# Linear attention and a gated feed-forward layer on one core: the same steps in another order, with more two-operand work on GpSimd

## The chip, the cores and the metric

The kernel runs on one core of one Trainium2 chip. Its time is the device time of one execution in microseconds (us), the median of several runs. Five engines share the work, and each takes its own instructions strictly in the order in which they were written: TensorE (PE, matrix products into PSUM), VectorE (DVE), ScalarE (ACT), GpSimd (POOL) and SyncE (SP, which here only issues transfers). An instruction that waits holds up everything behind it on its engine.

## The reference

The inputs are q, k, v of shape (8, 8, 576, 64), three weight matrices and a vector of 512 gains.

```
q_s = softmax(q, axis=-1)                      # over the 64 features of a head
k_s = softmax(k, axis=2)                       # over the 576 positions
kv  = einsum('bhsd,bhse->bhde', k_s, v)
att = einsum('bhsd,bhde->bhse', q_s, kv)       # -> x, (4608, 512)
xn  = x / sqrt(mean(x*x) + 1e-6) * rms_g
g   = xn @ w_gate                              # 512 -> 1536
out = (g * sigmoid(g) * (xn @ w_val)) @ w_out  # 1536 -> 512
```

All is float32. The kernel keeps the precision with 16-bit and reduced-precision products by splitting each operand into a high part (a cast) and a low part (the operand less its high part), and by adding three products of the parts.

## The kernel before

**Tiling.** The 4608 tokens are nine blocks of 512 (index j, 0 to 8). For every block the program computes the attention of its tokens in four groups of two heads (`q_...` steps, and for each of the eight sequences the `k_...`, `v_...` and `kv_...` steps), normalises the result (`n_...`, `x_nrm`), and sends it through the feed-forward layer. Blocks 0 and 1 are done in plain products (`f1`, `f1p`, `f2`), while the weights are loaded and converted. Blocks 2 to 8 use seven products in place of eight for a 2x2 split of the two input weight matrices, so sums and differences of quarters of the weights and of the tokens are formed first.

**The steps of a late block j**, by name:

- `n_rows.j` (L969) spreads the normalising factors over a tile, `x_nrm.j.g` (L849) multiplies four tiles by it, `x_sum.j.n` (L885 to L891) forms four sums of token quarters, `o_x_hi` casts them and `o_x_lo` (L905) forms the low parts. These are the moving operands of the seven products.
- `pp.j.u.n` (L1118) is one of the seven products for one of six slices u of the hidden width: 12 matmuls into one PSUM bank. There are only two such banks (pool `ps_gv`), so a product can start when the second-last one before it has been evicted.
- `ev.j.u.n` evicts and adds up: `ev` 0 on ScalarE, `ev` 1 to 6 on VectorE at L1137, `ev` 7 on VectorE at L1142; `ev` 8 and 9 are the two silu (L1145, ScalarE), `ev` 10 and 11 (L1148, VectorE) multiply gate and value, both then in SBUF.
- `hu_hi` (L402, ScalarE) and `hu_lo` (L1157) split the hidden values, `o_hi` (L402) and `o_lo` (L1000) the output weights. The tile of a low part is `hl` or `ol`, of a high part `hh` or `oh`.
- `fu.j.u.n.k` (L1170) adds the slice to the output, two matmuls each of (hh, oh), (hh, ol) and (hl, oh), in that order. `store` writes the block out.

Other steps that form a low part or a product of two tiles in SBUF are `q_sub` (L770), `q_mul` (L792), `q_lo` (L807), `x_acc` (L919), `n_lo` (L928), `w_lo` (L992), `b_lo` (L1073), `t_op` (L1081 to L1087), `t_lo` (L1099) and `h_lo` (L1228).

**What sets the order.** No loop and no scheduler at build time: a table of 3260 steps, `ORDER`, is read from first to last, and each step appends its instructions to its engines' queues. A step may carry a letter for its engine: `:A` ScalarE, `:D` VectorE, `:P` GpSimd. Many steps that read two operands from SBUF can run on either of the last two. All transfers are issued by SP, in the table's order.

```
    with tc.manual_schedule():
        for step in ORDER.split():
            step, _, engine = step.partition(":")
            name, *args = step.split(".")
            unit[0] = where[engine]
            steps[name](*map(int, args))
```

Of the kernel before, what the change touches and what calls it, by code (L numbers as in the profile page):

```python
# [23 lines left out]
exp_table constants k_load.0.0 q_load0.0.0 v_ones.0.0 kv_zero0.0 warm.9 v_ones.0.2 kv_zero0.1 k_load.0.2 v_ones.0.1  # L24
v_ones.0.3 v_load.0.0 kv_zero.4 kv_zero.5 warm.2.0 kv_zero.6 q_load0.0.3 k_max0.0.0 warm.2.1 kv_zero.7 warm.2.2
kv_zero.0 k_load.0.3 warm.2.10 kv_zero.1 q_max0.0.0 q_load0.0.1 kv_zero.2 k_tr.0.0 warm.2.11 k_top.0.0 kv_zero.3
warm.2.3 k_diag.0.0:A k_max0.0.2 q_sub0.0.0:P k_load.0.1 warm.2.12 v_load.0.2 k_rows.0.0 warm.2.5 k_sub.0.0 v_ones.1.0
v_ones.1.1 q_exp.0.0 warm.2.4 q_load0.0.2 warm.2.6 q_sum0.0.0 k_exp.0.0 warm.2.7 q_eps0.0.0 v_load.0.3 warm.2.8
q_rec0.0.0 q_max0.0.3 q_mul0.0.0:P k_mm.0.0 v_load.0.1 k_max0.0.3 k_tr.0.2 warm.2.9 q_sub0.0.3:P g_load k_top.0.2
k_tr.0.3 q_t0.0.0 load_w.0.0 k_eps.0.0 k_diag.0.2:A k_top.0.3 k_rec.0.0 load_w.0.1 q_exp.0.3 k_rows.0.2 q_max0.0.1  # L30
load_w.1.0 k_diag.0.3:A k_sub.0.2 q_sub0.0.1:P q_c0.0.0:A load_w.1.1 k_rows.0.3 k_load.1.0 kv_norm0.0.0:A k_max0.0.1
k_exp.0.2 k_sub.0.3 load_w.0.2 q_exp.0.1 k_mm.0.2 q_load0.1.0 q_sum0.0.3 k_exp.0.3 k_tr.0.1 q_x0.0.0 k_top.0.1
q_max0.0.2 k_diag.0.1:A k_mm.0.3 x_sq.0.0 load_w.2.0 q_sum0.0.1 q_sub0.0.2:P k_rows.0.1 load_w.2.1 n_sum0.0 k_eps.0.2
k_sub.0.1 load_w.1.2 q_exp.0.2 load_w.3.0 q_eps0.0.3 x_hi.0.0:A q_rec0.0.3 load_w.3.1 k_rec.0.2 q_mul0.0.3:P
q_eps0.0.1 load_w.3.2 k_eps.0.3 k_exp.0.1 x_lo.0.0 k_load.1.1 kv_norm0.0.2:A q_rec0.0.1 k_mm.0.1 k_rec.0.3
q_mul0.0.1:P q_sum0.0.2 conv_mul.0.0 q_t0.0.3 load_w.2.2 k_eps.0.1 conv_low.0.0.1 k_rec.0.1 conv_shift.0.0 q_t0.0.1
k_load.1.2 kv_norm0.0.3:A q_eps0.0.2 conv_sign.0.0 q_c0.0.3:A kv_norm0.0.1:A q_load0.1.1 q_rec0.0.2 q_x0.0.3
conv_add.0.0.1 g_abs conv_mul.0.1 q_c0.0.1:A conv_shift.0.1 q_mul0.0.2:P conv_low.0.1.1 q_x0.0.1 conv_sign.0.1
v_load.1.0 x_hi.0.3:A q_t0.0.2 conv_add.0.1.1 x_sq.0.3 x_lo.0.3 s_tr.0 x_sq.0.1 k_max.1.0 w_hi.0.0.2:A n_sum0.1
q_load0.1.2 s_top.0 q_c0.0.2:A f1.0.0.0.0 w_lo.0.0:P f1.0.1.0.0 w_lo.0.1:D s_rows.0 x_hi.0.1:A q_x0.0.2 s_bits.0  # L40
load_w.4.0 conv_low.1.0.2 f1.0.0.0.1 load_w.4.1 f1.0.1.0.1 q_max0.1.0 f1.0.1.0.3 v_load.1.1 f1.0.0.0.3 conv_mul.1.0
x_lo.0.1 q_sub0.1.0:P x_sq.0.2 conv_shift.1.0 x_hi.0.2:A n_sum0.2 conv_sign.1.0 conv_low.0.2.1 f1.0.0.0.2 x_lo.0.2
f1.0.0.1.0 conv_mul.1.1 n_sum0.3 q_exp.1.0 conv_shift.1.1 f1.0.1.0.2 f1.0.0.1.1 conv_low.2.0.2 conv_sign.1.1
f1.0.0.1.2 f1.0.1.1.0 f1.0.1.1.1 f1.0.0.1.3 n_t.0 conv_add.1.0.2 conv_mul.0.2 f1.0.0.2.0 f1.0.1.1.2 f1.0.0.2.1 n_y0.0
conv_low.1.2.1 f1.0.1.1.3 f1.0.0.2.2 conv_shift.0.2 f1.0.1.2.0 f1.0.1.2.1 f1.0.0.2.3 q_sum0.1.0 f1.0.1.2.2 f1.0.1.2.3
n_y1.0 w_hi.1.0.2:A load_w.5.0 load_w.5.1 conv_low.3.0.2 w_lo.1.0:P conv_sign.0.2 k_tr.1.0 n_rows.0 w_lo.1.1:P
conv_mul.2.0 k_top.1.0 conv_low.3.2.1 g_mul.0 conv_add.0.2.1 k_diag.1.0:A n_cols.0 f1.1.0 silu.0 q_eps0.1.0 q_rec0.1.0
k_max.1.1 load_w.4.2 q_mul0.1.0:P conv_low.2.2.1 q_load0.1.3 conv_shift.2.0 k_rows.1.0 h_mul.0 k_sub.1.0 f1.1.1
conv_sign.2.0 conv_mul.2.1 k_exp.1.0 g_mul.1 conv_shift.2.1 conv_mul.1.2 f2.0 silu.1 conv_sign.2.1 conv_shift.1.2
conv_mul.3.0 conv_add.2.0.2 conv_sign.1.2 conv_shift.3.0 conv_mul.3.1 conv_sign.3.0 conv_add.1.2.1 w_hi.2.0.2:A  # L50
load_w.6.0 h_mul.1 q_t0.1.0 load_w.6.1 q_max0.1.1 conv_low.4.0.2 w_lo.2.0:P f1.2.0 load_w.5.2 q_c0.1.0:D
conv_shift.3.1 conv_mul.3.2 w_lo.2.1:P k_max.1.2 q_sub0.1.1:P f1.2.1 conv_sign.3.1 conv_shift.3.2 q_exp.1.1
conv_add.3.0.2 conv_mul.2.2 g_mul.2 conv_low.5.0.2 conv_sign.3.2 f2.1 q_sum0.1.1 conv_mul.4.0 conv_add.3.2.1
load_w.7.0 conv_shift.2.2 w_hi.3.0.2:A load_w.7.1 conv_shift.4.0 load_w.7.2 conv_low.4.2.1 w_lo.3.0:P conv_sign.2.2
silu.2 conv_sign.4.0 k_mm.1.0 w_lo.3.1:P q_max0.1.2 conv_mul.4.1 f1.3.0 k_load.1.3 k_eps.1.0 h_mul.2 conv_add.2.2.1
conv_shift.4.1 k_rec.1.0 conv_low.6.0.2 v_ones.1.2 v_load.1.2 conv_sign.4.1 q_sub0.1.2:P f2.2 q_max0.1.3
kv_norm0.1.0:A conv_add.4.0.2 g_mul.3 conv_mul.4.2 load_w.6.2 q_eps0.1.1 conv_low.5.2.1 q_rec0.1.1 conv_shift.4.2
conv_mul.5.2 conv_sign.4.2 silu.3 q_sub0.1.3:P load_w.8.0 f1.3.1 conv_shift.5.2 w_hi.4.0.2:A load_w.8.1 conv_sign.5.2
conv_add.4.2.1 conv_mul.5.0 w_lo.4.0:D conv_low.7.0.2 w_lo.4.1:P conv_shift.5.0 load_w.8.2 q_x0.1.0 conv_sign.5.0
q_exp.1.2 conv_add.5.2.1 o_hi.4:A f1.4.0 q_sum0.1.2 conv_mul.5.1 h_mul.3 o_lo.4:P conv_low.7.2.1 load_w.10.2  # L60
conv_shift.5.1 o_hi.5:A conv_sign.5.1 q_exp.1.3 q_mul0.1.1:P f1.4.1 g_mul.4 conv_mul.6.0 o_lo.5:P q_sum0.1.3
q_load.2.0 silu.4 conv_shift.6.0 kv_hi.1.0:A x_sq.1.0 conv_add.5.0.2 conv_sign.6.0 conv_low.6.2.1 f2.3 h_mul.4
conv_mul.6.1 q_eps0.1.2 x_raw.1.0 conv_shift.6.1 h_hi.4:A conv_sign.6.1 kv_lo.1.0:P load_w.10.0 conv_mul.6.2 h_lo.4:P
q_rec0.1.2 load_w.10.1 s_max.0.0 w_hi.5.0.2:A k_tr.1.1 warm.2.13 conv_add.6.0.2 conv_low.8.0.2 k_top.1.1 f2.4
conv_shift.6.2 conv_sign.6.2 k_diag.1.1:A conv_low.8.2.1 w_lo.5.0:D conv_mul.7.0 w_lo.5.1:P s_max.2.0 w_hi.6.0.2:A
k_rows.1.1 f1.5.0 conv_add.6.2.1 k_sub.1.1 conv_low.10.2.1 k_max.1.3 k_exp.1.1 w_lo.6.0:P o_hi.6:A q_t0.1.1
conv_shift.7.0 o_lo.6:P f1.6.0 q_c0.1.1:D g_mul.5 conv_mul.7.1 w_lo.6.1:P conv_sign.7.0 silu.5 conv_low.10.0.2
conv_shift.7.1 q_mul0.1.2:P k_mm.1.1 conv_sign.7.1 f1.5.1 k_load.2.0 v_ones.1.3 k_eps.1.1 conv_mul.7.2 conv_add.7.0.2
# [1234 lines left out]
```

## Time and profile before

| | us |
|---|---|
| median of 3 runs (range) | 1038.28 (1038.12 to 1042.46) |
| the profiled execution | 1038.59 |
| its span, first to last instruction | 1036.8 |
| PE busy | 948.4 |
| VectorE busy | 860.3 |
| ScalarE busy | 594.7 |
| GpSimd busy | 460.2 |

The profile is of one execution. A row of a group view reads: line, engine, operation, written tile, read tiles, shapes, count, then total busy time and the mean of one in ns, then the idle time ahead of them and what ended it. A row of waits reads: engine and line that waited, engine and line waited for, total us, how many times, the longest. A row of the timeline reads: start, duration, engine, line, operation, tiles, count, and in brackets the engine's idle time ahead of it and what ended it. Lines are those of the kernel before; the table is one line longer in the changed kernel, so every line behind it there has a number higher by one.

### The profile page before, as it was taken

The numbers are of one execution on the slowest core, as the hardware profiler recorded it, in microseconds if no ns is written. First come the engines' busy times: TensorE is split into PE (matmuls) and PEld (weight loads), VectorE is DVE, ScalarE is ACT, GpSimd is POOL, SyncE is SP. The second block draws the span as 40 slices with busy tenths as digits, with TensorE's granted clock in tenths as the row PEclk, the third lists the DMA queues.
The fourth block names the chain that finished last, engine by engine and source line by source line (L and its number), as shares of the span: only waits on it lengthen the run. The fifth ranks groups of instructions, "written<-read, shape, count | busy, mean of one in ns | idle before, by whom it ended". The sixth has DMA issues, their size and how long they took to land.

```text
span 1036.8 us, 17459 instructions
## 1 busy us (share of the span) xinstructions
PE 948.4 (91%) x6418; PEld 735.5 (71%) x6418; DVE 860.3 (83%) x1564; ACT 594.7 (57%) x929; POOL 460.2 (44%) x386
## 2 busy tenths in 40 slices
...
DMA packets 129697, 57.82 MB, mean 56 GB/s; under 512 B 101796, under 2 KB 123596, under 8 KB 129612
## 3 DMA queue, kind: packets, MB, share of 16 engines
...
## 4 chain that ended last, share of the span: by engine, by line
DVE 39%; PE 34%; issue 6%; DMA 4%; ACT 4%; SPq 3%; POOL 1%; DVEq 0%; ACTq 0%
PE ps_gv L1118 19%; PE ps_o L1170 12%; SPq L687 3%; DVE w_br L1137 3%; DVE ol L1000 2%; DVE tm L1137 2%; DVE sw L759 2%; DVE x_raw L849 2%; DVE xo L905 2%; DMA qt<-in_q_dram 2%; DVE cm L562 1%; PE ps_gv L1197 1%; DVE wf L1137 1%; DVE w_br L1148 1%; DVE sm L778 1%
## 5 line engine op out<-in xcount | busy, mean ns | idle before, releaser
L1118 PEld LDWEIGHTS <-w_gv 128*128 128x128 f16 x2016 | 192.8, 99 | 47.6 <-issue 25.0
L1118 PE MATMUL ps_gv<-xo,w_gv 128*128 128x256 f16 x1296 | 157.8, 276 | 5.1 <-ACT xo L402 3.1
L402 ACT CAST oh<-w_o 128x512 fp32r<-128x512 f32 x104 | 64.1, 617 | 131.2 <-PE ps_o L1170 130.1
L1000 POOL TENSOR_TENSOR ol<-w_o,oh 128x512 fp32r<-128x512 f32 x44 | 57.7, 1311 | 129.1 <-ACT oh L402 128.8
L1170 PE MATMUL ps_o<-oh,hh 128*128 128x512 f32 x336 | 111.1, 412 | 3.2 <-ACT hh L402 3.2
L1170 PE MATMUL ps_o<-oh,hl 128*128 128x512 f32 x336 | 105.3, 394 | 2.4 <-DVE hl L1157 2.3
L1170 PE MATMUL ps_o<-ol,hh 128*128 128x512 f32 x336 | 105.2, 394 | 0.0
L1118 PEld LDWEIGHTS <-w_br 128*128 128x128 f16 x756 | 72.2, 98 | 25.8 <-issue 14.6
L1118 PE MATMUL ps_gv<-x_op,w_gv 128*128 128x256 f16 x720 | 87.4, 273 | 0.3 <-DVE tm L1137 0.3
L1000 DVE TENSOR_TENSOR ol<-w_o,oh 128x512 fp32r<-128x512 f32 x60 | 56.5, 942 | 37.3 <-ACT oh L402 37.3
L1185 PE MATMUL ps_gv<-xo,wf 128*128 128x512 f32 x288 | 76.5, 417 | 2.1 <-DVE tm L1212 2.0
L1170 PEld LDWEIGHTS ps_o<-oh,hl 128*128 128x128 f32 x336 | 62.7, 189 | 19.3 <-DVE hl L1157 5.2
L1118 PE MATMUL ps_gv<-xo,w_br 128*128 128x256 f16 x540 | 65.5, 273 | 9.8 <-DVE tm L1142 5.7
L1170 PEld LDWEIGHTS ps_o<-ol,hh 128*128 128x128 f32 x336 | 63.5, 189 | 14.3
L1118 PEld LDWEIGHTS <-wf 128*128 128x128 f16 x504 | 49.8, 101 | 29.2 <-issue 17.1
L1185 PEld LDWEIGHTS ps_gv<-xo,wf 128*128 128x128 f32 x288 | 55.1, 196 | 18.3 <-issue 2.7
L807 POOL TENSOR_TENSOR ql<-qT,qh 128x512 fp32r<-128x512 f32 x20 | 26.6, 1329 | 92.7 <-ACT qh L402 92.7
L1170 PEld LDWEIGHTS ps_o<-oh,hh 128*128 128x128 f32 x336 | 58.1, 190 | 12.6 <-ACT hh L402 3.5
L1137 DVE TENSOR_TENSOR tm<-ps_gv,tm 128x512 f32<-128x512 f32 x71 | 48.0, 682 | 12.1 <-PE ps_gv L1118 11.7
L1137 DVE TENSOR_TENSOR w_br<-ps_gv,w_br 128x512 f32<-128x512 f32 x71 | 48.0, 683 | 11.0 <-PE ps_gv L1118 10.9
L919 POOL TENSOR_TENSOR acc<-acc,sq 128x512 f32<-128x512 f32 x18 | 25.7, 1426 | 65.3 <-ACT sq L915 65.3
L1118 PE MATMUL ps_gv<-xo,wf 128*128 128x256 f16 x360 | 44.2, 276 | 9.3 <-DVE w_br L1142 3.3
...
## 6 DMA issues: line engine op xcount, KB each, us to landing
...
```

The costliest lines, as they stand in the source:

```text
L402: (e.copy if e is nc.scalar else e.tensor_copy)(dst, src)
L687: nc.sync.dma_start(qt[p0:p0 + 32, c0 // 32:c1 // 32], q[b, 2 * g + h, s0:s0 + c1 - c0, 32 * f:32 * f + 32].rearrange("(m c) i -> c m i", ...
L759: nc.vector.tensor_reduce(out=sw[32 * (a ^ 1):32 * (a ^ 1) + 32], in_=st[32 * a:32 * a + 32].unsqueeze(2), axis=AX.X, op=ALU.max)
L807: on(nc.gpsimd).tensor_tensor(out=ql, in0=qT_[j, g], in1=qh_[j, g][0].bitcast(F32), op=ALU.subtract)
L849: on(nc.vector).tensor_tensor(out=XR[:, g], in0=XR[:, g], in1=r_[j], op=ALU.mult)
L905: on(nc.gpsimd).tensor_tensor(out=x_as(j, m, xl), in0=x_part(j, m), in1=x_as(j, m, xo_[j, m][0]), op=ALU.subtract)
L919: on(nc.gpsimd).tensor_tensor(out=acc_[j], in0=acc_[j], in1=sq_[j, g], op=ALU.add)
L1000: on(nc.vector).tensor_tensor(out=ol, in0=WO_(s % NF), in1=wo_[s][0].bitcast(F32), op=ALU.subtract)
L1118: nc.tensor.matmul(pair(ps, i), lhsT=a[:, wt], rhs=y if i else y.rearrange("p (a c) -> p a c", a=2), start=(k == 0 and i == 0 and p == 0), ...
L1137: nc.vector.tensor_tensor(out=out, in0=b, in1=src[j, u], op=ALU.add)
L1170: nc.tensor.matmul(po[2 * n + t], lhsT=a[:, o:o + P], rhs=w, start=(u == 0 and i == 0 and p == 0), stop=(u == NU - 1 and i == 1 and p == 2))
L1185: nc.tensor.matmul(pd[s], lhsT=m[:, a, c * P:(c + 1) * P], rhs=X[j, c][x], start=(n == 1), stop=(n == 3 * NKT))
```

## The change

The steps are the same 3260, with the same arguments. Their order is new from the first row on, and some carry another letter. The order was written on the premise that the work of GpSimd and VectorE on two operands in SBUF uses one resource. No instruction is added to or removed from the computation itself. Of the diff, which replaces the whole table, the rows of one place (`...` where lines are left out):

```
-ev.5.5.2 n_rows.6 fu.5.4.1.1 ev.5.5.3 x_nrm.6.3:P x_nrm.6.1:D fu.5.4.0.0 x_nrm.6.0:D x_nrm.6.2:P q_t.7.1 o_x_hi.6.0
...
+pp.5.4.3 ev.5.4.9 ev.5.4.5 ev.5.4.11 pp.5.5.1 n_rows.6 ev.5.4.6 ev.5.5.0 x_nrm.6.2:P k_eps.7.0 pp.5.5.2 k_rec.7.0
+k_sub.7.1 kv_hi.7.0:A x_nrm.6.1:P kv_lo.7.0 k_exp.7.1 pp.5.5.6 ev.5.5.1 x_nrm.6.3:P k_top.7.2 ev.5.5.8 q_t.7.1
...
```

Counted over the table, the letters move as follows. A step with no letter runs on its default engine, the same in both.

| step | `:D` before, now | `:P` before, now |
|---|---|---|
| all | 254, 223 | 303, 334 |
| `hu_lo` (L1157) | 39, 11 | 45, 73 |
| `o_lo` (L1000) | 60, 57 | 44, 47 |
| `x_sum` (L885 to L891) | 1, 13 | 27, 15 |
| `x_nrm` (L849) | 16, 18 | 16, 14 |
| `t_op`, `t_lo` (L1081 to L1099) | 18, 9 | 30, 39 |
| `q_mul` (L792) | 24, 20 | 4, 8 |
| `b_lo`, `w_lo` (L1073, L992) | 16, 10 | 32, 38 |

ScalarE's queue gets 100 loads of an activation table in place of 82, since silu and exp alternate more often.

**Place 1: VectorE, the end of block 5 and the preparation of block 6.** The row at L1142 evicts the fourth product of slice 5 of block 5 and so frees a bank; r is the factor tile, x_raw the attention result, xo the low parts, ol a low part of the output weights. Before:

```order
L1137 TENSOR_TENSOR tm<-ps_gv,tm 128x512
L969 STREAM_TRANSPOSE r<-y 128x512
L1137 TENSOR_TENSOR w_br<-ps_gv,tm 128x512
L849 TENSOR_TENSOR x_raw<-x_raw,r 128x512 x2
L797 STREAM_TRANSPOSE qT<-qt 128x512
L905 TENSOR_TENSOR xo<-x_raw,xo 128x512
L1000 TENSOR_TENSOR ol<-w_o,oh 128x512
L905 TENSOR_TENSOR xo<-x_raw,xo 128x512
L1000 TENSOR_TENSOR ol<-w_o,oh 128x512
L1142 TENSOR_TENSOR w_br<-ps_gv,w_br 128x512
```

And in the changed kernel:

```order
L563 TENSOR_REDUCE cm<-kt 116x128
L1138 TENSOR_TENSOR w_br<-ps_gv,tm 128x512
L1143 TENSOR_TENSOR w_br<-ps_gv,w_br 128x512
L1149 SCALAR_TENSOR_TENSOR w_bx<-wf,ig,w_bx 128x512
L906 TENSOR_TENSOR xo<-sq,xo 128x512
L906 TENSOR_TENSOR xo<-x_raw,xo 128x512
L1158 TENSOR_TENSOR hl<-w_bx,hh 128x512
L1158 TENSOR_TENSOR hl<-tm,hh 128x512
L890 TENSOR_TENSOR sq<-sq,x_raw 128x512
L1138 TENSOR_TENSOR tm<-ps_gv,tm 128x512
```

The six two-operand instructions that stood between two evictions have left that place; the eviction at L1143 now follows its forerunner at once, and six others stand behind it, ahead of the next eviction.

**Place 2: VectorE, the same place one block later (end of block 6).** Before:

```order
L969 STREAM_TRANSPOSE r<-y 128x512
L1137 TENSOR_TENSOR tm<-ps_gv,w_bx 128x512
L849 TENSOR_TENSOR x_raw<-x_raw,r 128x512 x2
L797 STREAM_TRANSPOSE qT<-qt 128x512
L905 TENSOR_TENSOR x_op_94<-x_raw,x_op_94 128x512
L1000 TENSOR_TENSOR ol<-w_o,oh 128x512
L905 TENSOR_TENSOR xo<-x_raw,xo 128x512
L1000 TENSOR_TENSOR ol<-w_o,oh 128x512
L1142 TENSOR_TENSOR tm<-ps_gv,tm 128x512
```

And in the changed kernel:

```order
L1138 TENSOR_TENSOR tm<-ps_gv,w_bx 128x512
L906 TENSOR_TENSOR xo<-x_raw,xo 128x512 x2
L892 TENSOR_TENSOR sq<-x_raw,sq 128x512
L808 TENSOR_TENSOR ql<-qT,qh 128x512
L1001 TENSOR_TENSOR ol<-w_o,oh 128x512
L906 TENSOR_TENSOR xo<-sq,xo 128x512
L798 STREAM_TRANSPOSE qT<-qt 128x512
L1143 TENSOR_TENSOR tm<-ps_gv,tm 128x512
```

Here six two-operand instructions stand ahead of the eviction in both kernels; the factor tile and the multiplications by it have moved to an earlier place.

**Place 3: GpSimd, block 4, around the low parts of its slice 1** (hl with w_bx and tm). Before:

```order
L807 TENSOR_TENSOR ql<-qT,qh 128x512
L1157 TENSOR_TENSOR hl<-w_bx,hh 128x512
L558 MEMSET vt 116x10
L1000 TENSOR_TENSOR ol<-w_o,oh 128x512 x2
L919 TENSOR_TENSOR acc<-acc,sq 128x512
L1157 TENSOR_TENSOR hl<-w_br,hh 128x512
```

And in the changed kernel:

```order
L808 TENSOR_TENSOR ql<-qT,qh 128x512
L1158 TENSOR_TENSOR hl<-w_bx,hh 128x512
L1158 TENSOR_TENSOR hl<-tm,hh 128x512
L771 TENSOR_TENSOR qt<-qt,st 128x512
L1001 TENSOR_TENSOR ol<-w_o,oh 128x512
L920 TENSOR_TENSOR acc<-acc,sq 128x512
```

The second low part of the slice, which VectorE formed before, now stands behind the first one on GpSimd.

More of the change, by code (lines that the diff above doesn't have):

```diff
@@ L23 @@
 ORDER = """
[L24 to L68, printed above, removed]
```

547 lines of the change are left out of this document (296 added, 251 removed).

## The prediction, made before the changed kernel was run

> **What bounds the kernel now.** I read the busy times by stage first, then what TensorE waits for, then the timeline at the longest of those waits. Busy time of each engine in four stages:
>
> ```profile
> 0.00:150.00 150.00, 135.73 (x679) 97.93 (x680) 128.85 (x240) 114.41 (x173) 110.91 (x112) 0.97 0.66 183
> 150.00:350.00 200.00, 166.53 (x933) 106.25 (x932) 178.45 (x331) 140.81 (x219) 114.93 (x92) 0.92 0.18 42
> 350.00:850.00 500.00, 472.07 (x3603) 388.89 (x3601) 443.15 (x835) 280.97 (x442) 196.24 (x157) 0.99 0.16 38
> 850.00:1037.00 187.00, 174.03 (x1211) 142.40 (x1208) 109.83 (x160) 58.55 (x97) 38.15 (x27) 0.98 0.04 14
> sum 1037.00, PE 948.36 PEld 735.47 DVE 860.28 ACT 594.75 POOL 460.24; mean PE 237.09 PEld 183.87 DVE 215.07 ACT 148.69 POOL 115.06
> ```
>
> The columns are PE, PEld, DVE, ACT, POOL, then the granted clock. TensorE is the bound: busy 948.36 of 1037. A new order cannot shorten its matmuls, so all that can be won is its idle time, 88.6 us: 14.3 up to 150, 33.5 from 150 to 350, 27.9 from 350 to 850, 13.0 after that. VectorE is nearly full in the middle stages (178.45 of 200, 443.15 of 500), GpSimd is not. TensorE's own waits:
>
> ```profile
> PE ps_gv L1118 <- DVE tm L1142: 12.2, 7, 3.8
> PE ps_o L1244 <- ACT hh L402: 6.8, 1, 6.8
> PE ps_gv L1118 <- DVE w_br L1142: 5.3, 4, 3.3
> PE ps_gv L1118 <- DVE w_bx L1142: 4.1, 2, 3.3
> PE ps_gv L1118 <- ACT xo L402: 3.1, 1, 3.1
> PE ps_gv L1118 <- DVE wf L1142: 2.3, 3, 1.1
> PE ps_gv L1118 <- DVE xo L905: 2.1, 1, 2.1
> ```
>
> The reader is to see one line, L1142: the four rows that name it make 23.9 us in 16 waits. It is one eviction in each slice. Why is it late? VectorE, GpSimd and TensorE at the end of block 5:
>
> ```profile
> 714.17 3.12 DVE L849 TENSOR_TENSOR x_raw<-x_raw,r 128x512 f32<-128x512 f32 x2
> 717.97 1.28 DVE L905 TENSOR_TENSOR xo<-x_raw,xo 128x512 f16<-128x512 f32 x1
> 719.18 1.76 DVE L1000 TENSOR_TENSOR ol<-w_o,oh 128x512 fp32r<-128x512 f32 x1
> 720.86 1.64 DVE L905 TENSOR_TENSOR xo<-x_raw,xo 128x512 f16<-128x512 f32 x1
> 722.42 1.75 DVE L1000 TENSOR_TENSOR ol<-w_o,oh 128x512 fp32r<-128x512 f32 x1
> 724.09 0.68 DVE L1142 TENSOR_TENSOR w_br<-ps_gv,w_br 128x512 f32<-128x512 f32 x1
> ...
> 713.75 2.99 POOL L849 TENSOR_TENSOR x_raw<-x_raw,r 128x512 f32<-128x512 f32 x2 [1.73 <-DVE r L969]
> ...
> 720.35 1.60 POOL L905 TENSOR_TENSOR xo<-sq,xo 128x512 f16<-128x512 f32 x1
> ...
> 724.82 2.21 PE L1118 MATMUL ps_gv<-xo,wf 128*128 128x256 f16 x12 [3.27 <-DVE w_br L1142]
> ```
>
> Six two-operand instructions stand ahead of the eviction and take 3.12 + 1.28 + 1.76 + 1.64 + 1.75 = 9.55 us, while GpSimd works too. The same kinds a while earlier, when one engine has the field:
>
> ```profile
> 362.08 0.68 DVE L807 TENSOR_TENSOR ql<-qT,qh 128x512 fp32r<-128x512 f32 x1
> 360.32 1.83 DVE L1148 SCALAR_TENSOR_TENSOR tm<-w_bx,ig,tm 128x512 f32<-128x512 f32 x1
> ...
> 360.33 1.27 POOL L919 TENSOR_TENSOR acc<-acc,sq 128x512 f32<-128x512 f32 x1 [4.74 <-ACT sq L915]
> ```
>
> Alone, VectorE needs 0.68 and GpSimd 1.27. The VectorE instruction that started with GpSimd's at 360.3 took 1.83: it stood until the other was done. So the two engines do exclude one another on such work, and of the 9.55 us above 9.55 - 6 x 0.68 = 5.5 were lost to it, more than the 3.27 that TensorE waited. The groups show that this is general, and what it is tied to:
>
> ```profile
> L1000 DVE TENSOR_TENSOR ol<-w_o,oh 128x512 fp32r<-128x512 f32 x60 | 56.5, 942 | 37.3 <-ACT oh L402 37.3
> L849 DVE TENSOR_TENSOR x_raw<-x_raw,r 128x512 f32<-128x512 f32 x16 | 22.6, 1440 | 0.1
> L1148 DVE SCALAR_TENSOR_TENSOR tm<-tm,ig 128x512 f32<-128x512 f32 x19 | 21.0, 1103 | 0.8 <-ACT tm L1145 0.2
> L1137 DVE TENSOR_TENSOR w_br<-ps_gv,w_br 128x512 f32<-128x512 f32 x71 | 48.0, 683 | 11.0 <-PE ps_gv L1118 10.9
> ```
>
> Two SBUF operands: means of 942, 1440 and 1103 ns. One operand in PSUM, L1137: 683, no more than alone. The premise of the change is real in this trace.
>
> **The change part by part.**
>
> *Fewer instructions on VectorE.* The letter D goes from 254 to 223 steps: 31 x 0.68 = 21 us less VectorE work, 31 x 1.27 = 39 us more on GpSimd, which has 1037 - 460 us to spare. As such it is worth nothing, TensorE being the bound; its worth is in the terms that follow.
>
> *The transitions between blocks.* At the end of block 5 (place 1) the six instructions have gone from ahead of the eviction; the next eviction gets six instead. At the end of block 6 (place 2) six still stand ahead, but the multiplications have moved to where GpSimd multiplies nothing. TensorE's pace between such places, from the chain that ended last:
>
> ```profile
> 588.81 4.11 PE ps_o L1170 x18
> 592.91 1.32 PE ps_gv L1118 x12
> ```
>
> A `pp` of 12 matmuls is 1.3 us, an `fu` of six 1.4. Counted so, the factor row of blocks 3 to 8 stood 24, 24, 9, 9, 9 and 37 us of TensorE work ahead of the first product that needs it, and stands 8, 25, 25, 16, 25 and 38 ahead now: more room at three places, less at one. The waits on L1142 are 23.9 us. All could go, or none if the clusters only hold up the next eviction; I take half, as one of the two places shown keeps its cluster: -12 (ends -24 and 0).
>
> *The preparation of block 2* has the same pattern in the rows on xo (3.1 and 2.1): about half, -3 (ends -5 and 0).
>
> *The run-in before block 1's products.* TensorE's longest single wait, 6.8 us, and the chain that leads to it on VectorE:
>
> ```profile
> 166.85 3.31 DVE L849 TENSOR_TENSOR x_raw<-x_raw,r 128x512 f32<-128x512 f32 x2
> 170.09 3.32 DVE L1073 TENSOR_TENSOR w_br<-w_gv,w_br 128x512 f16<-128x512 f32 x2
> 173.33 3.33 DVE L905 TENSOR_TENSOR x_op<-x_raw,x_op 128x512 f16<-128x512 f32 x2
> 176.59 1.64 DVE L1228 TENSOR_TENSOR hl<-tm,hh 128x512 fp32r<-128x512 f32 x1
> ...
> 167.91 3.38 POOL L849 TENSOR_TENSOR x_raw<-x_raw,r 128x512 f32<-128x512 f32 x2
> 171.25 3.18 POOL L905 TENSOR_TENSOR x_op<-x_raw,x_op 128x512 f16<-128x512 f32 x2
> 174.39 1.72 POOL L1085 TENSOR_TENSOR w_gv<-w_gv 128x512 f32<-128x512 f32 x1
> ```
>
> Seven instructions take 11.6 us for 7 x 0.68 = 4.8. The new order leaves five there, but puts 5 us of reductions and key work ahead of them and moves an output step of the old kernel, which filled part of this gap, behind it. 0 (ends -5 and +5).
>
> The Trainium skill (SBUF — State Buffer, "Who interferes with whom") has VectorE's second SBUF operand come through an interface that it shares with GpSimd, locked for a whole instruction. The single 1.83 us row agrees; in the long stretch above a pair took about 1.6 us, not the 0.68 + 1.27 = 1.95 that a strict lock would make of it. By the lock a contended instruction costs VectorE 1.27 more, by the rows 0.9 more, and the -12 would be -17.
>
> *Other evictions and the silu path, 350 to 850.* After the L1142 rows some 10 us of idle time are left there, spread over waits under 1 us. VectorE's relief may take a part: -4 (ends -10 and +5).
>
> *Low parts on GpSimd.* 28 `hu_lo` move from VectorE to GpSimd, mostly as the second of a pair (place 3): each ends 1.27 - 0.68 = 0.6 us later. What covers it is that an `fu` step needs hl only for its last two of six matmuls. At 4.11/18 = 0.23 us each that is 0.9 us of cover, and the sibling `fu` of 1.4 us ahead of it. Uncovered it would cost 28 x 0.6 = 17. I take +2 (ends 0 and +17). What stands behind them on GpSimd is mostly `o_lo`, which has 6 us and more of TensorE work ahead of its reader.
>
> *Activation tables.* The loads go from 82 to 100:
>
> ```profile
> L1145 ACT ACT_TABLE_LOAD x26 | 33.4, 1283 | 0.5
> ```
>
> 18 x 1.283 = 23 us on ScalarE, which is idle for 442 us. They stand ahead of exp and silu; a silu has 1.3 us and more of TensorE work behind it. +1 (ends 0 and +12, half of them bare).
>
> *Transfers* move on SP's queue too. VectorE waits for them rarely,
>
> ```profile
> DVE st L753 <- DMA qt<-in_q_dram: 10.4, 7, 3.5
> ```
>
> and the load of q stands about as far ahead of its reader as before: 0 (ends -4 and +4).
>
> **The sum:** -12 - 3 + 0 - 4 + 2 + 1 + 0 = -16. The profiled execution took 1038.59 with a span of 1036.8, so 1022.6; the median of the runs shown is 1038.28, the same within 0.3. I predict 1022.
>
> **The rivals.**
>
> *All that contention costs comes back.* If the new places fit as meant, the L1142 waits (24), block 2's (5) and half the rest of the middle (5) go, and the clock of 0.92 in the second stage rises with fewer gaps: 1038 - 34 = 1004. For it: L1137 shows what uncontended work takes. Against it: six-instruction clusters remain, and 31 instructions run at 1.27 for 0.68.
>
> *The wait only moves.* The two banks still hang on VectorE, the clusters now delay the eviction after, and TensorE waits there: 1037. For it: place 1 has as many instructions behind the eviction as stood ahead of it.
>
> *GpSimd's pair becomes the late one (slower).* At place 3 both low parts are GpSimd's: 0.62 for the cast, then 2 x 1.27, 3.2 us in all, against 0.62 + 1.27 and VectorE in parallel before. It decides from the point at which the second hl comes later than 0.9 us after its `fu` began; if the casts come late, all 28 are bare: +17, and GpSimd's longer chains hold VectorE's two-operand steps, so that the -12 isn't had. 1022 + 17 + 12 = 1051. Against it: before, TensorE's waits for hl were 2.3 us in 5 times,
>
> ```profile
> PE ps_o L1170 <- DVE hl L1157: 2.3, 5, 1.2
> ```
>
> with 45 of 84 of these on GpSimd already.
>
> *The pair as the bound (slower).* Taken as one resource, the exclusive work grows by 31 x (1.27 - 0.68) = 18 us. Where the two engines' joint work is what ends last, the time grows by that: 1038 + 18 = 1056. Against it: GpSimd's 196 of 500 us in the long stage leave room. The Trainium skill (Perfetto Trace Analysis, "Optimizing Scalar/DVE Operations") warns of just this, that moving work between the two might not help.
>
> *The change does not do what it says* I rule out: the queues differ as the places show.
>
> **How the numbers follow.** Forecast 0.53, all back 0.15, the wait only moves 0.15, GpSimd's pair 0.12, the pair as bound 0.05. Half a per cent, 5 us, is about what a measurement of this kernel tells from no change. So faster 0.68, same 0.15, slower 0.17. The forecast's own range is 1010 to 1032. To hold 8 in 10 it takes in most of the full return and the unmoved case, and half of the way to the slower ones: 1002 to 1043.
>
> **What would show it.** Right: means near 0.7 us for L1000, L849 and L1148 on VectorE, fewer waits on the eviction that was at L1142, busy time of TensorE unchanged near 948. Wrong: those means as high as before (the new order didn't part the engines), or low with TensorE idle as long, on hl from GpSimd, on silu, or on another eviction.

## The result, and the profile after

The changed kernel took 1003.96 us (median of 4 runs, 998.00 to 1008.04) beside 1038.30 (1038.12 to 1042.46) for the kernel before on the same chip: a ratio of 0.9656, 95% interval 0.9600 to 0.9711. The forecast was 1022, in a range of 1002 to 1043; the gain of 34 us is about twice the forecast 16 and is the size that the first rival gave (1004). The profiled execution took 1005.23 with a span of 1003.5. Executions of the changed kernel spread more than those of the old one; four more, taken later, lay between 998.91 and 1014.92, with a median of 1010.75 beside the old kernel's 1040.49 of that time. Their ratio, 0.9645 (0.9593 to 0.9696), goes by fast runs alone and leaves out the two longest, 1014.41 and 1014.92, which count as slow because they are over 1.5% above the fastest. The median of all eight is 1006. What causes a part of the spread is told below.

Busy time by stage, with the columns of the same view before (PE, PEld, DVE, ACT, POOL, granted clock):

```profile
0.00:150.00 150.00, 130.57 (x648) 94.65 (x650) 126.45 (x228) 113.27 (x170) 110.88 (x111) 0.95 0.65 181
150.00:350.00 200.00, 175.18 (x1028) 114.53 (x1026) 160.83 (x315) 149.07 (x228) 115.94 (x101) 0.93 0.19 44
350.00:850.00 500.00, 487.85 (x3718) 407.30 (x3717) 416.95 (x856) 306.78 (x471) 216.76 (x184) 1.00 0.16 39
850.00:1004.00 154.00, 144.58 (x1034) 119.59 (x1032) 86.96 (x137) 47.91 (x79) 29.14 (x23) 0.99 0.04 15
sum 1004.00, PE 938.18 PEld 736.07 DVE 791.19 ACT 617.02 POOL 472.71; mean PE 234.55 PEld 184.02 DVE 197.80 ACT 154.26 POOL 118.18
```

VectorE is the engine that changed: 860.28 to 791.19, 69 less, of which fewer steps explain 21 (the prediction's 31 x 0.68). GpSimd gained 31 steps, 39 us by the prediction's count, and is busy only 12 longer. Between 350 and 850, TensorE's idle time fell from 27.9 to 12.2, and more matmuls fit into the same 500 us (3718 for 3603). TensorE's busy time fell as well, by 10.2 over the whole span, which the prediction had excluded. So of the 33 us by which the span is shorter, 23 come from TensorE's idle time and 10 from shorter matmuls. What TensorE waits for now:

```profile
PE ps_gv L1198 <- DVE x_op L906: 5.3, 2, 3.8
PE ps_gv L1198 <- DVE tm L1208: 4.1, 3, 2.0
PE ps_a L620 <- ACT kt L612: 3.8, 1, 3.8
PE ps_gv L1119 <- DVE tm L1138: 3.8, 7, 0.9
...
PE ps_gv L1119 <- DVE w_br L1143: 1.2, 2, 0.8
...
PE ps_gv L1119 <- DVE tm L1143: 0.7, 1, 0.7
...
PE ps_o L1171 <- POOL hl L1158: 0.5, 1, 0.5
...
PE ps_gv L1119 <- DVE wf L1143: 0.5, 1, 0.5
```

The eviction that was L1142 is L1143 here: 23.9 us of waits before, 2.4 now. The wait for low parts from GpSimd, on which the prediction put +2, is 0.5. The chain of work that ended last has changed hands too. Its shares of the span by engine, from the page before and then from the page after:

```profile
DVE 39%; PE 34%; issue 6%; DMA 4%; ACT 4%; SPq 3%; POOL 1%; DVEq 0%; ACTq 0%
PE 53%; DVE 16%; ACT 10%; issue 5%; POOL 4%; DMA 1%; SPq 1%; DVEq 0%; ACTq 0%; POOLq 0%
```

In the old kernel this chain ran over VectorE (39%) more than over TensorE (34%). The prediction didn't use this row. The groups that the prediction had named:

```profile
L1001 DVE TENSOR_TENSOR ol<-w_o,oh 128x512 fp32r<-128x512 f32 x57 | 42.4, 744 | 50.3 <-ACT oh L403 49.7
L850 DVE TENSOR_TENSOR x_raw<-x_raw,r 128x512 f32<-128x512 f32 x18 | 12.9, 760 | 0.1
L1149 DVE SCALAR_TENSOR_TENSOR tm<-tm,ig 128x512 f32<-128x512 f32 x19 | 14.9, 786 | 0.5
```

Means of 942, 1440 and 1103 ns have become 744, 760 and 786, near the 680 that an instruction takes alone. At the end of block 5, the place of the prediction's timeline, VectorE and then GpSimd now read:

```profile
698.03 0.68 DVE L1138 TENSOR_TENSOR w_br<-ps_gv,tm 128x512 f32<-128x512 f32 x1
699.35 0.69 DVE L1143 TENSOR_TENSOR w_br<-ps_gv,w_br 128x512 f32<-128x512 f32 x1 [0.64 <-PE ps_gv L1119]
699.96 0.74 DVE L1149 SCALAR_TENSOR_TENSOR w_bx<-wf,ig,w_bx 128x512 f32<-128x512 f32 x1
...
692.03 4.96 POOL L850 TENSOR_TENSOR x_raw<-x_raw,r 128x512 f32<-128x512 f32 x4 [3.12 <-DVE r L970]
697.07 1.29 POOL L886 TENSOR_TENSOR sq<-x_raw 128x512 f32<-128x512 f32 x1
700.17 1.54 POOL L906 TENSOR_TENSOR xo<-x_raw,xo 128x512 f16<-128x512 f32 x1 [1.81 <-ACT xo L403]
```

GpSimd does all four multiplications in one row, 4 x 1.24, while VectorE does evictions from PSUM, a transpose and reductions (0.69 an eviction). Here VectorE waits 0.64 for TensorE ahead of L1143; before, TensorE waited 3.27 for VectorE. At the end of block 6 (place 2) six two-operand instructions still stand ahead of the eviction, but GpSimd idles beside them:

```profile
798.80 1.28 DVE L906 TENSOR_TENSOR xo<-x_raw,xo 128x512 f16<-128x512 f32 x2
800.00 0.68 DVE L892 TENSOR_TENSOR sq<-x_raw,sq 128x512 f32<-128x512 f32 x1
...
804.36 1.27 POOL L1001 TENSOR_TENSOR ol<-w_o,oh 128x512 fp32r<-128x512 f32 x1 [5.97 <-ACT oh L403]
```

**Where the gain lies.** TensorE does the same matmuls in nearly the same order, so the two traces can be set side by side at equal matmul work (each matmul counted at its full-speed duration, 0.11 us for the products and 0.23 for `fu`, as in the prediction's chain rows; with another weight for the small matmuls single entries move by up to some 2 us). The table shows how much later each kernel's profiled execution reaches the same work than the kernel before; the kernels in its lower rows are the experiments below.

| work done, us | 200 | 240 | 350 | 400 | 450 | 550 | 650 | 750 | 800 | 900 |
|---|---|---|---|---|---|---|---|---|---|---|
| reached before, at us | 271 | 323 | 435 | 487 | 543 | 646 | 752 | 860 | 917 | 1019 |
| changed kernel | +1.0 | -4.8 | -1.2 | -2.0 | -9.5 | -15.6 | -19.7 | -26.1 | -31.6 | -31.7 |
| e13_no_row | -4.2 | -10.7 | -7.3 | -8.0 | -15.6 | -21.3 | -25.3 | -31.8 | -37.3 | -37.5 |
| e11_splice | -2.3 | -10.0 | -6.5 | -7.3 | -14.8 | -20.6 | -25.0 | -31.4 | -36.9 | -37.1 |
| e14_splice_late | +1.0 | +4.2 | +6.9 | +6.1 | -1.4 | -7.2 | -11.0 | -17.4 | -22.9 | -23.0 |
| e12_splice_back | +6.0 | +33.7 | +33.8 | +33.4 | +33.7 | +33.5 | +36.0 | +35.3 | +36.1 | +36.2 |
| e4_x_on_dve | +4.3 | +0.2 | +1.7 | +1.6 | +2.5 | +0.2 | -2.5 | -5.2 | -7.6 | -7.6 |

The changed kernel gains in six steps of 4 to 8 us, at the entries to block 2 and to blocks 4 to 8, and nothing ahead of the first (+1.0 at 200). The entry to block 3, which begins at 412 us in the old kernel, brings no gain. It is also the one block whose factor row the prediction counted nearer to its first product than before (8 us of TensorE work for 24); no run tested whether that is the reason.

### The profile page after: what moved, and what is told of

Same layout as the page of the kernel before. It is cut to its first block, busy times and chain, and to the rows that moved or that the text cites. A ratio compares the mean times of both kernels' runs of the same rounds, so it can differ in the third digit from the quotient of the medians.

```text
span 1003.5 us, 17504 instructions
## 1 busy us (share of the span) xinstructions
PE 938.2 (93%) x6418; PEld 736.1 (73%) x6418; DVE 791.2 (79%) x1533; ACT 617.0 (61%) x947; POOL 472.7 (47%) x417
## 4 chain that ended last, share of the span: by engine, by line
PE 53%; DVE 16%; ACT 10%; issue 5%; POOL 4%; DMA 1%; SPq 1%; DVEq 0%; ACTq 0%; POOLq 0%
PE ps_gv L1119 28%; PE ps_o L1171 19%; DVE tm L1138 2%; PE ps_gv L1198 1%; PE ps_a L819 1%; ACT L612 1%; DVE w_br L1138 1%; ACT L775 1%; POOL w_gv L481 1%; PE ps_a L620 1%; DVE sw L760 1%; DVE kt L608 1%; POOL wf L993 1%; PE ps_gv L1186 1%; PE ps_o L1245 1%
## 5 line engine op out<-in xcount | busy, mean ns | idle before, releaser
L1119 PE MATMUL ps_gv<-xo,w_gv 128*128 128x256 f16 x1296 | 153.7, 273 | 3.9 <-ACT tm L403 1.9
L1001 POOL TENSOR_TENSOR ol<-w_o,oh 128x512 fp32r<-128x512 f32 x47 | 62.5, 1330 | 114.7 <-ACT oh L403 114.3
L1001 DVE TENSOR_TENSOR ol<-w_o,oh 128x512 fp32r<-128x512 f32 x57 | 42.4, 744 | 50.3 <-ACT oh L403 49.7
L1186 PEld LDWEIGHTS ps_gv<-xo,wf 128*128 128x128 f32 x288 | 55.9, 198 | 17.4 <-ACT w_o L462 3.1
L1158 POOL TENSOR_TENSOR hl<-tm,hh 128x512 fp32r<-128x512 f32 x24 | 31.1, 1302 | 67.2 <-ACT hh L403 54.1
L1158 POOL TENSOR_TENSOR hl<-w_br,hh 128x512 fp32r<-128x512 f32 x25 | 31.9, 1279 | 53.2 <-ACT hh L403 25.2
```

What stands on the lines that cost most here:

```text
L1001: on(nc.vector).tensor_tensor(out=ol, in0=WO_(s % NF), in1=wo_[s][0].bitcast(F32), op=ALU.subtract)
L1119: nc.tensor.matmul(pair(ps, i), lhsT=a[:, wt], rhs=y if i else y.rearrange("p (a c) -> p a c", a=2), start=(k == 0 and i == 0 and p == 0), ...
L1158: on(nc.gpsimd).tensor_tensor(out=hl, in0=G_[j, u, n], in1=h_[j, u, n][0].bitcast(F32), op=ALU.subtract)
L1186: nc.tensor.matmul(pd[s], lhsT=m[:, a, c * P:(c + 1) * P], rhs=X[j, c][x], start=(n == 1), stop=(n == 3 * NKT))
```

## The experiments

Theory: at the change of blocks VectorE, not TensorE, sets the pace, and what it loses to GpSimd there is what the new order brings back. The rivals were that the gain is TensorE's clock, that the letters alone or the order alone bring it, and that it is made somewhere else.

To follow VectorE's loss, a second quantity is worked out for each trace: the sum, over VectorE's instructions, of the duration beyond what an instruction of the same form takes undisturbed (the tenth lowest in a hundred of its group; at most 0.75 us for two operands of 128x512). It is 127 us before and 77 after. Around the six steps (290 to 340, 480 to 540, 600 to 640, 710 to 740, 810 to 850 and 885 to 920 us of the old kernel, chosen after the table was seen) the loss is 47 us before and 16 after, and the same matmul work takes 255 us before and 218 after; outside them the changed kernel is 3 us slower. VectorE's busy time there falls by 44, so some 13 us of it are work that now stands elsewhere, and not loss.

**Letters alone and order alone.** `e1_letters` keeps the old order and takes the changed kernel's letters (219 steps differ), `e2_order` the reverse. A row of the old table and the same row of `e1_letters`, as an example:

```
-ev.5.5.2 n_rows.6 fu.5.4.1.1 ev.5.5.3 x_nrm.6.3:P x_nrm.6.1:D fu.5.4.0.0 x_nrm.6.0:D x_nrm.6.2:P
+ev.5.5.2 n_rows.6 fu.5.4.1.1 ev.5.5.3 x_nrm.6.3:P x_nrm.6.1:P fu.5.4.0.0 x_nrm.6.0:P x_nrm.6.2:P
```

> The order of before, the letters of the changed kernel: 31 two-operand steps fewer on VectorE, but every step stays where it was. Theory A (parting in time: the gain comes from VectorE's and GpSimd's two-operand instructions no longer coinciding where blocks meet): the coincidences stay, so 1030 to 1045. Theory B (the letters: VectorE is relieved of 31 instructions): at least half of the gain, 1021 or less. Theory C (room: the tokens of the next block are prepared with more TensorE work ahead of their first product): as before, 1036 to 1040.

> The order of the changed kernel, the letters of before. A: two-operand steps that stood on one engine in a row are mixed on both again, so part of the gain is lost: 1012 to 1030, with means near 1 us for the contended VectorE lines. B: hardly any gain left, 1030 to 1038. C: the whole gain stays, 1000 to 1008.

Letters alone: 1064.56, ratio 1.0226 (1.0196 to 1.0256), 25 us slower. Order alone: 1034.58, 0.9946 (0.9928 to 0.9964), 5 us faster. VectorE's loss is 100 and 99 us, half way for each. The first time lies above all three ranges that were expected, the second above that of theory A and in that of B, which the first run excludes. With the letters alone, TensorE waits for low parts from GpSimd, a row of `e1_letters`:

```profile
PE ps_o L1170 <- POOL hl L1157: 9.2, 14, 1.3
```

and with the order alone the L1143 waits come to 10.2 us, most of it in these two rows of `e2_order`:

```profile
PE ps_gv L1119 <- DVE w_br L1143: 4.8, 3, 2.0
PE ps_gv L1119 <- DVE tm L1143: 3.3, 4, 1.3
```

So neither half is worth much, and one alone is a loss: the 34 us come from both together. In the six stretches above, the order alone takes 232 us for 255, with a loss of 28, but gives 16 of these 23 us back outside them. The letters alone take 257 though VectorE's loss there falls to 32: a smaller loss is worth nothing while something else comes late. What the prediction's rival "GpSimd's pair becomes the late one" says is real in the old order and gone in the new. The rest of what `e1_letters` loses, 10 of it ahead of block 2, wasn't taken apart; its trace has there one of the long holds described below, 5.81 us at 142.7.

**TensorE's clock.** After the 3.27 us wait at 724.82 that the prediction shows, the 12 matmuls of a product took 2.21 us, for 1.47 in other rows of this view. The granted clock was 0.50 behind it (busy times of a stretch of the kernel before, the clock is the third number from the end):

```profile
725.40:728.80 3.40, 3.35 (x18) 2.05 (x16) 3.25 (x6) 0.63 (x2) 2.61 (x2) 0.50 0.04 8
```

`e3_fill` adds 24 matmuls with a result that nobody reads in three of these waits, so that TensorE doesn't stand still:

```
+    def fill(j, n):
+        for _ in range(n):
+            nc.tensor.matmul(pm_[j][:, 2 * P:], lhsT=mean_w, rhs=mean_w.unsqueeze(1).broadcast_to([P, 2, P]),
+                             start=True, stop=True)
-pp.4.5.3
+fill.5.24 pp.4.5.3
```

> The order and letters of before, with 24 useless matmuls (256 columns, into a dead PSUM tile) ahead of the product that waits 3.3 to 3.8 us at the end of blocks 4, 5 and 6. The waits themselves stay. Before, the granted clock was 0.5 for 3.4, 3.4 and 6.8 us after those three waits. If the slow clock after a wait is a cost of its own, TensorE gains half of 13.6 us: 1031 to 1034. If only the wait counts, nothing changes: 1037 to 1040.

It took 1039.60, ratio 1.0001 (0.9984 to 1.0019): no change. Yet the clock was mended: over the span its mean rose from 0.970 to 0.975 (0.977 in the changed kernel), and a stretch and TensorE's timeline of `e3_fill` show it at two of the three places:

```profile
726.00:730.00 4.00, 3.21 (x30) 2.50 (x28) 3.82 (x8) 1.04 (x3) 2.76 (x2) 1.00 0.01 1
```

```profile
616.20 3.10 PE L1177 MATMUL ps_a<-mean_w 128*128 128x256 f32 x24
...
619.77 1.47 PE L1118 MATMUL ps_gv<-x_op,wf 128*128 128x256 f16 x12 [0.46 <-DVE w_bx L1142]
...
725.01 1.47 PE L1118 MATMUL ps_gv<-xo,wf 128*128 128x256 f16 x12 [0.45 <-DVE w_br L1142]
```

The matmuls take 1.47 for 2.21 and start at 725.01 for 724.82, and the kernel is no faster. So at these places TensorE's waits and its slow matmuls are both slack behind VectorE. A part of the 10 us by which TensorE's busy time fell in the changed kernel can be read so: with the waits gone, stretches at half clock are gone, but they had not set the time. That reading is not tested by itself.

**What a microsecond of VectorE is worth there.** In `e6_pad_before` and `e6_pad_after`, four reductions with one SBUF operand stand ahead of seven evictions. They were planned as 17 us in all; in the traces the 28 take 0.68 each, 19 in all:

```
+    def pad(n):
+        t = small.tile([P, T], F32, name="pad", bufs=1)
+        for _ in range(n):
+            nc.vector.tensor_reduce(out=t, in_=ones.unsqueeze(1).broadcast_to([P, T, P]), axis=AX.X, op=ALU.max)
-ev.5.5.7
+pad.4 ev.5.5.7
```

> The kernel before, with four reductions of one SBUF tile (0.6 us each, 2.4 us in all, one operand) put on VectorE ahead of the eviction at L1142 of the last slice of each of blocks 2 to 8: seven places, 17 us of VectorE work. The fill run showed that waking TensorE in the three long waits wins nothing, so the theory is now that VectorE, not TensorE, sets the time where blocks meet. Then at least five of the seven places pass it on in full: +10 to +17, 1049 to 1056. If TensorE is the bound there and the wait is an accident of one row, most of it hides: 1038 to 1045.

> The changed kernel with the same four reductions at the same seven evictions. If the new order has given VectorE slack where blocks meet, less is passed on than in the kernel before: +0 to +8, 1004 to 1012. If VectorE is as tight there as before, +10 to +17, 1014 to 1021.

In the old kernel: 1061.18, ratio 1.0194 (1.0168 to 1.0220), 21 us for 19, more than was expected. In the changed one: 1018.95, 0.9778 (0.9762 to 0.9794) of the old one, 13 more than the median of its eight and in the range expected if VectorE is as tight there as before. The largest L1142 rows of `e6_pad_before` are

```profile
PE ps_gv L1118 <- DVE tm L1142: 17.4, 6, 6.6
PE ps_gv L1118 <- DVE w_br L1142: 13.0, 6, 6.1
PE ps_gv L1118 <- DVE w_bx L1142: 9.1, 3, 6.0
```

for 12.2, 5.3 and 4.1 before. So VectorE's time passes on to the end about one for one in the old kernel. Most of it does in the changed one too: its evictions are on time, but with little to spare.

**The token steps.** `e4_x_on_dve` is the old kernel with all of the multiplications, sums and low parts of blocks 2 to 8 (`x_nrm`, `x_sum`, `o_x_lo`) on VectorE; 66 of 105 change. `e9_x_on_dve_after` does the same to the changed kernel (51 of 105), and `e8_x_letters` gives these three kinds of step the old kernel's letters in the new order (52 differ).

```
-x_nrm.6.3:P x_nrm.6.1:D x_nrm.6.0:D x_nrm.6.2:P
+x_nrm.6.3:D x_nrm.6.1:D x_nrm.6.0:D x_nrm.6.2:D
```

> The order and letters of before, except that all x_nrm, x_sum and o_x_lo of blocks 2 to 8 are on VectorE, so that GpSimd does nothing where blocks meet (70 of 105 instructions or so change hands). If the two engines exclude one another there (A), the help of GpSimd was worth next to nothing: VectorE does about 14 instructions of 0.6 us (8.5 us) in place of six in 9.6, and the time is 1032 to 1044. If the 1.6 us of the contended rows have another cause and GpSimd's help counts, VectorE's path grows by 8 x 0.68 = 5.4 us at each of six transitions: 1065 or more.

> The changed kernel, with the letters of before for x_nrm, x_sum and o_x_lo alone (52 steps differ). Giving all letters back cost 31 us. If it is the mixing of the engines where blocks meet that costs (A), these steps carry most of it: 1018 to 1034. If it is the relief of VectorE elsewhere (hu_lo, o_lo, B), little is lost: 1002 to 1010.

> The changed kernel with all x_nrm, x_sum and o_x_lo of blocks 2 to 8 on VectorE (51 of 105 change hands). In the order of before the same edit won 10 us, since GpSimd's part cost VectorE more than it took off it. If the new order has parted the two engines, GpSimd's part is a help there now and giving it up costs: 1012 to 1030. If VectorE still loses as much to GpSimd as it is relieved by, 998 to 1008.

`e4_x_on_dve` took 1029.32, ratio 0.9888 (0.9868 to 0.9909): VectorE got 66 instructions more and the kernel became 10 us faster, 3 below the expected range. Its loss fell from 127 to 94, in the six stretches from 47 to 14, where the same work takes 242 us for 255. GpSimd's help with these steps was worth less than nothing in the old order. In the new one it is worth something: 1012.80, 0.9730 (0.9685 to 0.9775), for `e9_x_on_dve_after`, 7 above the changed kernel's eight. At equal work its profiled execution ends 31.9 ahead of the old kernel, 5.6 less than `e13_no_row`, which like it has none of the long holds described below. `e8_x_letters` took 1019.78, 0.9817 (0.9780 to 0.9855), 14 above the changed kernel's eight, and VectorE's loss is back at 99. (Its profiled execution was its slowest, 1026.68, and holds one such hold of 6 us more than the changed kernel's first trace, so some 6 of the 99 are that.) So where these three kinds of step run is some 14 of the 34 us in the new order.

**The low parts of the hidden values.** `e5_hl_letters` gives 40 `hu_lo` their old letters back in the changed kernel.

```
-hu_lo.2.0.1:P
+hu_lo.2.0.1:D
```

> The changed kernel, with the letters of before for hu_lo alone (40 differ, 28 more of them on VectorE). The prediction priced their move to GpSimd as a small loss. If so, giving them back changes nothing or wins a little: 998 to 1006. If they are where VectorE's relief comes from (B), 1012 to 1030. If only the parting where blocks meet counts (A), 1002 to 1012.

1008.46, ratio 0.9699 (0.9684 to 0.9713). That is 4.5 us above the first median of the changed kernel and 2 below its second: the move to GpSimd shows no cost beyond the spread, and may have brought up to 4.

**The price of contention, by itself.** `e7_probe` is the old kernel with a measurement behind its last store: rows of 12 VectorE and 8 GpSimd instructions on 128x512, alone and at once, in one execution. (With two operands or a copy, VectorE's row outlasts GpSimd's and runs alone at the end.)

```
+        for kind in kinds:      # two SBUF operands, one in PSUM, a reduction, a copy
+            for n in range(12):
+                kind(n)
+            for n in range(8):
+                add(G, g[n % 4], x, y)
```

> The kernel before with a measurement appended after the last store: instructions of 128x512 float32, VectorE alone, GpSimd alone, then both at once with VectorE reading two SBUF operands, one from PSUM and one from SBUF, one SBUF operand in a reduction, one in a copy, and last GpSimd writing only (memset) against two SBUF operands. If two SBUF operands on VectorE against a reading GpSimd are what excludes, the first joint stretch shows VectorE near 1.6 us or more an instruction, the PSUM, reduction and memset stretches 0.6 to 0.7. The copy is not told by any row so far: 0.6 to 0.7, or as the first. The time grows by the appended stretches, 70 to 110 us.

Its timeline behind 1036 us; the first two rows are each engine alone:

```profile
1036.29 4.88 DVE L1179 TENSOR_TENSOR w_o<-x_raw 128x512 f32<-128x512 f32 x8
1042.47 8.57 POOL L1179 TENSOR_TENSOR w_o<-x_raw 128x512 f32<-128x512 f32 x7
...
1051.51 15.84 DVE L1179 TENSOR_TENSOR w_o<-x_raw 128x512 f32<-128x512 f32 x12 [0.28 <-POOL w_o L1190]
1051.55 13.44 POOL L1179 TENSOR_TENSOR w_o<-x_raw 128x512 f32<-128x512 f32 x8
...
1067.69 7.27 DVE L1179 TENSOR_TENSOR w_o<-ps_a,x_raw 128x512 f32<-128x512 f32 x12 [0.28 <-POOL w_o L1190]
...
1077.66 7.20 DVE L1181 TENSOR_REDUCE pr<-x_raw 128x1 f32<-128x512 f32 x12
...
1088.35 12.63 DVE L1182 COPY w_o<-x_raw 128x512 f32<-128x512 f32 x12 [0.28 <-POOL w_o L1190]
1088.40 11.30 POOL L1179 TENSOR_TENSOR w_o<-x_raw 128x512 f32<-128x512 f32 x8
...
1101.33 7.32 DVE L1179 TENSOR_TENSOR w_o<-x_raw 128x512 f32<-128x512 f32 x12 [0.28 <-POOL w_o L1196]
```

Alone, VectorE does one in 0.61 us (4.88 / 8) and GpSimd one in 1.22 (8.57 / 7). At once, eight pairs took 13.44: 1.68 a pair. VectorE alone would do the two instructions of a pair in 1.22. So two operands from SBUF on both engines at once are slower than all of it on VectorE, and GpSimd's part of a contended pair costs VectorE 1.07 us. With one operand in PSUM, with a reduction, or beside GpSimd's memsets (3.8 of the last row's 7.32 us), VectorE keeps its 0.61 (7.27, 7.20 and 7.32 for 12). A plain fp32 copy from SBUF to SBUF is held as well: eight pairs in 11.30, 1.41 each, for 0.33 alone (the last four, 12.63 - 11.30). The Trainium skill (SBUF — State Buffer, "Who interferes with whom") names the same operations as held and as free; with its lock held for a whole instruction a pair would take, as an estimate from these rows, 0.61 + 1.22 = 1.83, and the row's 1.68 decides.

**Whether all of it lies behind the start of block 2.** `e11_splice` has the old order and letters up to the first `f1p.18` step (some 235 us), then the new ones; `e14_splice_late` cuts at the first product of block 2 (304 us); `e12_splice_back` has the new ones up to there and then the old.

```
# e11, e14: the old table up to the cut, then those steps of the new table that are still to be done, in its order
# e12:      the new table up to the cut, then the rest of the old
```

> The order of before up to the seventh hidden slice of block 1 (about 235 us), and the changed kernel's order for all that is left then. TensorE's progress in the changed kernel was 1 to 5 us behind up to there, and ahead only after 300 us. If the gain lies in the block transitions alone, it stays whole: 998 to 1008, perhaps 1 to 3 us better than the changed kernel. If the later stages need what the new order prepares earlier, 1010 to 1025.

> The changed kernel's order and letters up to the first product of block 2 (about 300 us), the old ones behind it. Theory (the gain is VectorE's lost time at the block transitions, all of it behind this point): no gain, 1035 to 1045, the waits on the L1142 eviction back near 24 us. Rival (a good part of the gain is made in blocks 0 and 1, and only hidden in the comparison of the two traces at equal matmul work): 1015 to 1028.

> The reverse cut at the same place: the old kernel's order up to the first product of block 2, the changed one's behind it. Theory: it lacks the changed run-in and the first step of about 7 us at the entry of block 2, and keeps five of the six transitions: 1004 to 1012. Rival (the gain needs blocks 0 and 1 too): 1020 or more.

`e11_splice` took 1002.08 (999.93 to 1005.78), ratio 0.9640 (0.9613 to 0.9666): the whole gain without the new beginning. `e14_splice_late` took 1016.21, 0.9780 (0.9753 to 0.9808), and `e12_splice_back` 1071.94, 1.0303 (1.0254 to 1.0353). Neither of the last two lies in a range that was expected. Both have a seam, where steps that one table does early meet readers that the other has early. The seam shows as one long wait of TensorE, 27.2 us in `e12_splice_back`

```profile
PE ps_o L1245 <- DVE hl L1229: 27.2, 1, 27.2
```

and 8.8 us, the longest of three, in this row of `e14_splice_late`:

```profile
PE ps_gv L1119 <- ACT tm L403: 10.2, 3, 8.8
```

Behind the seam the table above is plain. `e12_splice_back`, with the old order, stays at +33.4 to +36.2 from block 2 to the end, and its four rows of L1143 waits are 12.6 + 5.0 + 4.1 + 2.4 = 24.1 again, for 23.9 in the old kernel. `e14_splice_late`, with the new order, goes from +6.9 to -23.0: 29.9 us in the entries to blocks 4 to 8, as the changed kernel does from -1.2 to -31.7 (30.5). The sixth step, into block 2, is the 6 to 8 us between 200 and 240 that the changed kernel and `e11_splice` have and `e14_splice_late`, which has its seam there, lacks.

**The spread.** `e10_after_again` is the changed kernel unaltered, with four more executions and another trace.

> The changed kernel itself once more, so that the other two timed here have it beside them on the same chip: 998 to 1008.

Its median, 1010.75, lies above that range. Its profiled execution took 1014.41. One small instruction of VectorE, 128 partitions x 8 numbers, took 0.93 us in the first trace of the changed kernel,

```profile
93.99 0.93 DVE L721 TENSOR_SCALAR sm<-sm 128x8 f32<-128x8 f32 x1
```

and 5.89 in this one, with TensorE's wait for what stands behind it:

```profile
93.95 5.89 DVE L721 TENSOR_SCALAR sm<-sm 128x8 f32<-128x8 f32 x1
...
PE ps_a L588 <- DVE w_o L476: 5.2, 1, 5.2
```

In both traces GpSimd has an unbroken row of work there, in the same places within 0.1 us. A second such hold is in both; here in the first trace, VectorE and then GpSimd:

```profile
141.47 6.08 DVE L920 TENSOR_TENSOR acc<-acc,sq 128x512 f32<-128x512 f32 x1
147.47 0.81 DVE L608 TENSOR_TENSOR kt<-kt,ps_a 116x640 f32<-116x640 f32 x1
...
140.71 2.60 POOL L481 TENSOR_TENSOR w_o<-w_o,w_br 128x512 int32<-128x512 int32 x2
143.25 1.30 POOL L993 TENSOR_TENSOR wf<-w_gv,wf 128x512 fp32r<-128x512 f32 x1
144.50 1.28 POOL L1229 TENSOR_TENSOR hl<-tm,hh 128x512 fp32r<-128x512 f32 x1
145.73 1.27 POOL L993 TENSOR_TENSOR wf<-w_gv,wf 128x512 fp32r<-128x512 f32 x1
```

VectorE's instruction was let in only when GpSimd's row ended at 147.0, past four of its instructions. `e13_no_row` takes both away: the sum of squares `x_acc.1.2` goes to GpSimd, and `q_eps0.1.3` with its reciprocal is written behind the row.

```
-w_hi.6.0.2:A q_eps0.1.3 q_rec0.1.3 conv_mul.7.2
+w_hi.6.0.2:A conv_mul.7.2
-k_top.1.1
+q_eps0.1.3 q_rec0.1.3 k_top.1.1
-x_acc.1.2:D
+x_acc.1.2:P
```

> The changed kernel with two edits: the sum of squares x_acc.1.2, which stood 6 us beside an unbroken row of GpSimd instructions, goes to GpSimd, and the small step q_eps0.1.3 with its reciprocal, which stood 5.9 us in some executions, is written behind that row. Theory (the spread of the changed kernel, 998 to 1015, comes from these two places): 996 to 1002 in every execution. Rival (the spread has another cause): runs spread over 10 us or more, as before, median 1000 to 1012.

1001.03 (998.51 to 1003.96), ratio 0.9628 (0.9594 to 0.9661), the best of all. At equal work its profiled execution is 5.8 us ahead of the changed kernel's from 150 us on, to the end (-37.5 for -31.7): the size of the hold at 141.47. Its four executions lie within 5.5 us where the eight of the changed kernel spread over 17. The upper end of that spread is explained by the holds as far as these three traces show. The expected 996 to 1002 in every execution wasn't met by one of the four, and the rest of the spread stays open.

## Why the prediction was wrong by half

- **What bounds the kernel.** "TensorE is the bound ... all that can be won is its idle time" is the step that failed. TensorE has the most busy time, but at the entries to the late blocks VectorE sets the pace: there the time didn't change when TensorE's clock was mended (`e3_fill`), rose by 21 for 19 us of reductions on VectorE (`e6_pad_before`), and fell by 10 when VectorE was let alone by GpSimd though it got more to do (`e4_x_on_dve`). The matmuls did get shorter, 948.4 to 938.2, which the step had ruled out: 10 of the 33 us came so, and 23 from idle time.
- **The transitions, -12.** The right mechanism and the mis-sized term. It took TensorE's wait on one eviction (23.9) and half of it. What counts at a place that VectorE paces is what VectorE loses, and the prediction had that number in hand: 5.5 us at the end of block 5, noted there as "more than the 3.27 that TensorE waited" and then not used. Six entries at 5.5 are 33; those into blocks 4 to 8 measured 30.5, with the one into block 2 some 6 more, and VectorE's loss at the six together fell by 31 (47 to 16). That 5.5 taken from one place comes so near is in part luck, since 13 us of other work left these places too. "Half, as one of the two places shown keeps its cluster" was wrong as well: six two-operand instructions are still in VectorE's queue there, but GpSimd idles beside them for 5.97 us, and it is the pair that costs.
- **The preparation of block 2, -3.** 6 to 8 by the table. VectorE's loss there fell from 8 to 4, so a part has the same reason.
- **The run-in, 0, ends -5 and +5.** +1.0 at 200 us of work in the profiled execution with its hold of 6 us, -4.2 in `e13_no_row` without it: inside the ends.
- **Other evictions, -4.** Not seen as a gain of its own. Between 240 and 350 us of work, around the entry to block 3, the changed kernel gives 3.6 back.
- **Fewer instructions on VectorE, "as such worth nothing".** This hung on the same premise. With the order alone 29 of the 34 us are missing (`e2_order`), so where work runs matters as much as when.
- **Low parts on GpSimd, +2.** Nothing, or up to 4 gained (`e5_hl_letters`); TensorE's wait is 0.5 us. The rival that feared them shows only with the old order (9.2 us in `e1_letters`).
- **Activation tables +1, transfers 0.** Not tested apart. Among TensorE's waits in the changed kernel no row on a silu or a transfer came up; the 3.8 us on an exp (L612) stand right behind the hold at 141.47.
- **The rivals.** "All that contention costs comes back" had the time, 1004, and its condition, that the L1142 waits go. Of the prediction's own signs the means near 0.7 and the fewer waits on L1142 came, the unchanged busy time of TensorE (948) didn't. Not all came back: VectorE still loses 77 us by the sum above. Its price, 24 + 5 + 5, counts only TensorE's waits, where 10 us came from the matmuls, and the clock of the second stage, which was to rise, went from 0.92 to 0.93 only. So the hit on 1004 is in part luck. "The wait only moves" and "the pair as the bound" didn't come.
